# Attention and MoE on one core: scores for two token tiles at once, scale sums with 16-bit operands

## The chip, the core and the metric

The kernel runs on one core of a Trainium2 chip. The core has a matrix engine (TensorE, PE in the profile, its weight loads PEld), a vector engine (VectorE, DVE), an engine for functions and copies (ScalarE, ACT), a general one (GpSimd, POOL), and SyncE (SP), which here only issues DMAs. Each engine takes its instructions in order; semaphores order them among each other. Matmuls write PSUM, a small memory of eight banks. The metric is the device time in microseconds, the median of three runs.

## What is computed

```python
def _attn_ref(q, k, v, sampled_blocks):      # B, H, S, D = 4, 8, 768, 64; blocks of 32 tokens
    scores = 1/sqrt(D) * q @ k^T
    mask = near the diagonal | first/last block row or column | sampled blocks
    scores = where(mask, scores, -1e9)
    attn = exp(scores - max) ; attn /= sum(attn) + 1e-9
    return attn @ v

def _moe_ref(x, w_in, w_out, alpha):         # 3072 tokens, 512 -> 2048 -> 512
    h = x @ w_in
    g = max(h, 0) + alpha * min(h, 0)
    return g @ w_out
```

The output of the attention, heads side by side, is the input x of the second part. All inputs are float32.

## The kernel before

**High and low halves.** A float32 operand is scaled by a power of two and split into a 16-bit high part and a 16-bit low part, the rest. Three of the four products of two such operands are summed (high by high, high by low, low by high); the scores take all four. The power of two comes from a sum of squares: ACT squares and sums along the row (L379), a matmul with a matrix of ones (L472 for k, L549 for v, L859 and L868 for the two weights) adds over the 128 rows, and DVE cuts the result to its exponent (`pow2`, L370). These small matmuls have float32 operands.

**Attention.** A chunk is two tiles of 128 tokens of one batch element; a unit is a chunk and a pair of heads; a step is one tile and one head. There are 12 chunks, 48 units and 192 steps, four steps to a unit. For a unit `T["qt"]` holds q transposed: for each head and tile 128 rows, the upper 64 the high part and the lower 64 the low part of the 64 features (`q_pair`, L453, and `emit_q_hi`, `emit_q_lo`, L441 and L446, which write them side by side). `T["kt"]` holds k in the same way, `T["ks"]` with the halves swapped. `emit_s` (L577) makes the 128 by 768 scores of a step: q by kt gives high by high plus low by low, q by ks gives both cross products, each in two matmuls of 512 and 256 columns into one buffer of two PSUM banks. The pool `s` has two such buffers, used also by the value products (`emit_av`, L649) and the mask. DVE then adds the mask and takes the minimum (L596), ACT does the exponential (L603), the result is split (L383, L387, L391, L393, L394), transposed by a DMA that SP issues (L624), and multiplied with v; the 64 columns of each of two heads make one half of the value product's 128 output rows.

**MoE.** For each chunk eight blocks of products with w_in (`emit_up`, L1023), the activation on DVE (L1033, L1034), its split on ACT (L1039) and POOL (L1044), and products with w_out (`emit_down`, L1065). Before its first block all 32 tiles of weights have to be loaded, converted and scaled. They come as float32 and are brought to an integer layout first in three steps: `emit_n1` on DVE (L829), `emit_n2` on ACT (L834) or DVE (L836), `emit_n3` on DVE (L841).

**Order.** Every piece of work is an `Op` with a priority, a price in microseconds for each engine that may run it, and the buffers it takes and gives back. `Plan.run` (L101) plays the engines forward, gives each ready op, in order of priority, to the engine that minimises its wait plus `PREF` times its price, and so fixes engine and order of all instructions before the kernel is built. An op starts only when all buffers that it takes are free. The constants at the top (L28 to L37, L47) set priorities: `MOE_LAG` is how many steps the MoE work of a chunk is behind its attention, `LDP` how far ahead of its use a weight tile is loaded, `V_WA`, `W_WA`, `V_WB`, `W_WB` when weights are prepared, `PL_V` and `P_V` when v is loaded and split. `attend` (L749) makes the ops of a step, `values` (L774) those of a value product, `raw_to_f32` (L948) those of the weights' conversion.

Of the kernel before, what the change touches and what calls it, by code (L numbers as in the profile page):

```python
# [14 lines left out]
ALU = mybir.AluOpType  # L15
# [9 lines left out]
GSCALE = 2.0**-20  # L25
SB = 205 << 23
SIZES0 = [2, 2, 2]
MOE_LAG = 13.782  # L28
EARLY = 15.72
MOE_BOOST = 0.564  # L30
V_WA = -18.766
W_WA = 0.725
V_WB = 0.937
W_WB = 0.741
LDP = 18.136
PL_V = -22.686
P_V = -0.023  # L37
PL = "gv"
LD = 4
P_PE = 0  # L40
# [3 lines left out]
HALF = 0  # L44
WO_PE = 1
LEADL = 2
PREF = {"PE": 1.0, "DVE": 1.91, "ACT": 1.15, "POOL": 0.744, "SP": 1.0}  # L47
SLOW = 1.25
UNTIL = 140.0
Q_PE = 1  # L50
# [167 lines left out]
def attn_moe(ctx: ExitStack, tc: tile.TileContext, q, k, v, sampled, w_in, w_out, alpha, out):  # L218
# [21 lines left out]
    def wt(tag, shape, dt, name=None):  # L240
        return work.tile(shape, dt, tag=tag, name=name or tag, bufs=bufs[tag])
# [9 lines left out]
    def new_small(name, dt=F32, w=1, n=4):  # L251
        return sm.tile([P, w], dt, tag=name, name=name, bufs=n)

    ident = cpool.tile([P, P], F32, name="ident")
    make_identity(nc, ident)
    ones = cpool.tile([P, P], F32, name="ones")
    nc.vector.memset(ones, 1.0)
    warm = cpool.tile([P, 1], F32, name="warm")
    nc.scalar.activation(warm, ones[:, 0:1], AF.Exp)
# [70 lines left out]
    bias = cpool.tile([P, NT, S], BF16, name="bias")  # L330
    ident16 = cpool.tile([P, P], F16, name="ident16")
    nc.gpsimd.tensor_copy(ident16, ident)
    nident = cpool.tile([P, P], F16, name="nident")
    nc.gpsimd.tensor_scalar(nident, ident, -1.0, None, ALU.mult)

# [75 lines left out]

    kbuf, ksbuf, vbuf, qtbuf, ptbuf, xbuf = {}, {}, {}, {}, {}, {}
    o_av = {}
    o_s, o_kt, o_ks, o_v2, o_qt, o_cs, o_pt, o_x, o_sv = {}, {}, {}, {}, {}, {}, {}, {}, {}

    def load(e, dst, src):
        (nc.sync if e == "SP" else nc.scalar).dma_start(dst, src)
# [21 lines left out]
        nc.vector.tensor_scalar(cs, T["rk", b][:, a:z], T["uq", c], -(2.0**-100), ALU.mult, ALU.min)  # L439

    def emit_q_hi(e, c):  # L441
        n = chunks[c][2]
        T["qn", c] = wt("qn", [P, H * n, 2, D], F16)
        times(e, T["qn", c][:, :, 0, :], T["qf", c].rearrange("p h t d -> p (h t) d"), T["sq", c])

    def emit_q_lo(c):  # L446
        nat = T["qn", c]
        nc.vector.scalar_tensor_tensor(
            nat[:, :, 1, :], T["qf", c].rearrange("p h t d -> p (h t) d"), T["sq", c], nat[:, :, 0, :],
            ALU.mult, ALU.subtract,  # L450
        )

    def q_pair(u):  # L453
        c, hp = units[u]
        n = chunks[c][2]
        return T["qn", c][:, 2 * hp * n : 2 * (hp + 1) * n].rearrange("p g a d -> p g (a d)")

    def emit_q_t(u):
        n = chunks[units[u][0]][2]
# [3 lines left out]
        )  # L463

    def emit_k_sq(b, hp):
        T["kss", b, hp] = new_small("kss")
        squares(T["kf", b, hp].rearrange("p h e -> p (h e)"), T["kss", b, hp])

    def emit_k_norm(b, hp):
# [76 lines left out]
    def lane_max(tot, key):  # L546
        pool, tag, w = key
        bc = pool.tile([P, w], F32, tag=tag, name="bc")
        nc.tensor.matmul(bc[:, :P], tot.broadcast_to([P, P]), ident, start=True, stop=True)  # L549
        return bc  # L550

    def emit_v_tot(b):
        T["vtot", b] = new_small("vtot")
        nc.vector.tensor_reduce(T["vtot", b], T["vss", b], AX.X, ALU.add)

    def emit_v_bc(b):
# [20 lines left out]
    def emit_s(n):  # L577
        u, j = steps[n]
        c, hp = units[u]
        b, t0, w = chunks[c]  # L580
        h, i = divmod(j, w)
        T["sp", n] = ps_s.tile([P, S], F32, tag="s", name="sp")
        for x, key in ((0, "kt"), (1, "ks")):
            kt = T[key, b, hp].rearrange("p h t j -> p h (t j)")
            for a, z in ((0, 512), (512, S)):
                nc.tensor.matmul(  # L586
                    T["sp", n][:, a:z], T["qt", u][:, h, i, :], kt[:, h, a:z], start=(x == 0), stop=(x == 1)
                )

    def emit_bias(n):  # L590
# [89 lines left out]
    def prep_k(b, hp, prio, gate, pl):  # L680
        fb = plan.buf("vf")
        o = plan.op(pl, LQ, lambda e: emit_load_kv(e, ("kf", b, hp), k_nat[b][:, 2 * hp : 2 * hp + 2, :]),
                    gate, [fb], dma=1.3)
        o = plan.op(prio, {"ACT": 0.85}, lambda: emit_k_sq(b, hp), [o], [], [fb])
        ab = plan.buf("o" if b == 0 else "h")
        o = plan.op(prio - 4, {"PE": 0.5}, lambda: emit_k_norm(b, hp), [o], [ab])
        o = plan.op(prio - 4, {"DVE": 0.35}, lambda: emit_k_scale(b, hp), [o], [], [ab])
        T["o_rk", b, hp] = o
        nb = plan.buf("ph")
        o = plan.op(prio, MAX4, lambda e: emit_k_hi(e, b, hp), [o], [nb], [fb])  # L690
        o = plan.op(prio, LOW4, lambda e: emit_k_lo(e, b, hp), [o], [], [nb, fb])
        kbuf[b, hp], ksbuf[b, hp] = plan.buf("kt"), plan.buf("ks")
        if b == 0 and hp < K_PE:
            for x, d, kb in ((0, o_kt, kbuf), (1, o_ks, ksbuf)):
                d[b, hp] = []
                for h in range(2):
                    tb = plan.buf("o")
                    t = plan.op(prio - 2, {"PE": 0.4 + 0.4 * x}, lambda x=x, h=h: emit_k_pe(b, hp, x, h), [o], [tb, kb[b, hp]], [nb])
                    d[b, hp].append(plan.op(prio - 2, {"ACT": 0.85, "DVE": 0.9}, lambda e, x=x, h=h: emit_k_copy(e, b, hp, x, h), [t], [kb[b, hp]], [tb]))
            return  # L700
        o_kt[b, hp] = [plan.op(prio - 2, {"SP": 2.0}, lambda: emit_k_t(b, hp), [o], [kbuf[b, hp]], [nb], dma=2.3)]
        o_ks[b, hp] = [plan.op(prio - 2, {"SP": 1.5}, lambda e: emit_k_swap(e, b, hp), o_kt[b, hp],
                               [ksbuf[b, hp]], [kbuf[b, hp]], dma=1.3)]

    def prep_v(b, pl, prio, gate):
        fbs, sq = [], []
        for hp in range(NP):
            fb = plan.buf("vf")
            fbs.append(fb)
            o = plan.op(pl + 0.1 * hp, LQ,  # L710
                        lambda e, hp=hp: emit_load_kv(e, ("vf", b, hp), v_nat[b][:, 2 * hp : 2 * hp + 2, :]),
                        gate, [fb] + ([plan.buf("ld")] if b == 0 else []), dma=1.3)
            sq.append(plan.op(pl + 2 + 0.1 * hp, {"ACT": 0.85}, lambda hp=hp: emit_v_sq(b, hp), [o], [], [fb]))
        o = plan.op(prio - 4, {"DVE": 0.1}, lambda: emit_v_tot(b), sq)
        ab = plan.buf("o" if b == 0 else "h")
        o = plan.op(prio - 4, {"PE": 0.6}, lambda: emit_v_bc(b), [o], [ab])
        o_sv[b] = plan.op(prio - 4, {"DVE": 0.5}, lambda: emit_v_scale(b), [o], [], [ab])
        for hp in range(NP):
            vbuf[b, hp] = plan.buf("v2")
            p = prio + hp  # L720
            o = plan.op(p, MAX4, lambda e, hp=hp: emit_v_hi(e, b, hp), [o_sv[b]], [vbuf[b, hp]], [fbs[hp]])
            o_v2[b, hp] = plan.op(p, LOW4, lambda e, hp=hp: emit_v_lo(e, b, hp), [o], [], [vbuf[b, hp], fbs[hp]])

    def prep_q(c, prio, pl, gate):
# [7 lines left out]
        for a, z in [(a, a + 1) for a in range(NP)] if c == 0 else [(0, NP)]:  # L732
            o = plan.op(prio, {"DVE": 0.15}, lambda a=a, z=z: emit_cs(c, a, z), [sc] + [T["o_rk", b, hp] for hp in range(a, z)])
            for hp in range(a, z):
                o_cs[us[hp]] = o
        o = plan.op(prio, {"POOL": 0.3 + 1.1 * f, "ACT": 0.2 + 0.9 * f, "DVE": (0.1 + 0.57 * f, 0)},
                    lambda e: emit_q_hi(e, c), [sc], [nb], [fb])
        lo = plan.op(prio, {"DVE": (0.1 + 1.15 * f, 0)}, lambda: emit_q_lo(c), [o], [], [nb, fb])
        for u in us:
            p = prio if c == 0 else first[u] - 5  # L740
            qtbuf[u] = plan.buf("qt")
# [7 lines left out]
    def attend(n):  # L749
# [1 line left out]
        c, hp = units[u]  # L751
        b, t0, w = chunks[c]
        h, i = divmod(j, w)
        sb, eb, pb = plan.buf("s"), plan.buf("e"), plan.buf("ph")
        o_s[n] = o = plan.op(n, {"PE": 0.66}, lambda: emit_s(n), [o_qt[u], o_av.get(steps[max(n - 3, 0)][0] - 2)] + o_kt[b, hp] + o_ks[b, hp], [sb],
                             [qtbuf[u], kbuf[b, hp], ksbuf[b, hp]])
        o = plan.op(n - 1, {"DVE": 0.94}, lambda: emit_bias(n), [o, o_cs[u], o_bias[t0 + i]], [eb], [sb])
        o = plan.op(n - 1, {"ACT": 0.94}, lambda: emit_exp(n), [o], [], [eb])
        o = plan.op(n - 2, {"DVE": 0.3}, lambda: emit_rs(n), [o])
# [32 lines left out]
    ssc = cpool.tile([P, NG], F32, name="ssc")  # L792
    gsc_a = cpool.tile([P, NG // 2], F32, name="gsc_a")
    am1_a = cpool.tile([P, NF // 2], F32, name="am1_a")
    isum = cpool.tile([P, NG], F32, name="isum")
    osum = cpool.tile([P, NG], F32, name="osum")
    s_wi = cpool.tile([P, 1], F32, name="s_wi")
    s_wo = cpool.tile([P, 1], F32, name="s_wo")
    s_wia = cpool.tile([P, 1], F32, name="s_wia")
# [147 lines left out]

    def raw_to_f32(name, f, p, o, deps, bufs):  # L948
        o = plan.op(p, {"DVE": (0.4, 0)}, lambda: emit_n1(name, f, 0), [o] + deps, [], bufs)
        o = plan.op(p, {"ACT": 0.7, "DVE": (0.64, 0)}, lambda e: emit_n2(e, name, f, 0), [o], [], bufs)  # L950
        return plan.op(p, {"DVE": (0.64, 0)}, lambda: emit_n3(name, f, 0), [o], [], bufs)

    def prep_wi(f, p):
# [6 lines left out]
        hb = plan.buf("h")  # L960
        o = plan.op(p - 2, {"PE": 0.9}, lambda: emit_gram("wi", g), [n3wi[f - 1], n3wi[f]], [hb])
        o = plan.op(p - 2, {"DVE": 0.28}, lambda: emit_gram_max("wi", g), [o], [], [hb])
        o = plan.op(p - 2, {"PE": 0.4}, lambda: emit_g_norm(g), [o], [], [hb])
        gs.append(plan.op(p - 2, {"DVE": 0.27}, lambda: emit_g_scale(g), [o], [], [hb]))
        prev = o_wi.get(f - 2)
        sb = plan.buf("sid")
# [7 lines left out]
    def prep_wo(f, p):  # L974
# [10 lines left out]
            return  # L985
        x = f // HF
        hb = plan.buf("h")
        o = plan.op(p - 3, {"PE": 0.6}, lambda: emit_o_norm(x), osq[-HG:], [hb])
        o = plan.op(p - 3, {"DVE": 0.3}, lambda: emit_o_scale(x), [o], [], [hb])
        o_swo.append(o)  # L990
        if WO_PE > x:
# [158 lines left out]
    for b in range(B):  # L1150
# [8 lines left out]
        for c in cb:  # L1159
# [52 lines left out]
```

## Time and profile before

| | |
|---|---|
| median of three runs | 863.18 us (862.94 to 869.0) |
| profiled execution, its own time | 860.22 us |
| its span, first to last instruction | 858.2 us |
| mean granted TensorE clock | 0.974 |
| up products L1023, busy | 266.7 us, 2304 matmuls |
| down products L1065, busy | 374.4 us summed over both kinds, 1152 matmuls |
| scores L586, busy | 150.8 us, 768 matmuls |
| value products L659, busy | 109.0 us, 1728 matmuls |

A time on the page is that of one profiled execution. Busy times of one engine may overlap: a matmul's record lasts until its result has drained, while the next has long begun, so the spacing of the starts is what a stream of matmuls costs. A group's row gives line, engine, operation, output and inputs, shapes, count, busy time, mean of one in ns, and the idle time ahead of it with what ended that.

### The profile page before, as it was taken

How to read it: one execution, taken by the hardware profiler on the slowest of the kernel's cores; microseconds unless marked ns; L12 is line 12 of the kernel's file. 1: busy time of each engine (PE TensorE's matmuls, PEld its weight loads, DVE VectorE, ACT ScalarE, POOL GpSimd, SP SyncE). 2: the span in 40 equal slices, each digit the busy share in tenths (PEclk: the TensorE clock that was granted, in tenths of full speed). 3: DMA queues.
4: the chain of work that ended last, by engine and by line, in shares of the span. 5: the costliest groups of instructions: out<-in, count | busy, mean ns of one | idle time of the engine just before them, and what ended most of it. 6: DMA issues, size and time to landing. Idle time of an engine off the chain costs nothing.

```text
span 858.2 us, 16828 instructions
## 1 busy us (share of the span) xinstructions
PE 805.6 (94%) x6291; PEld 541.2 (63%) x6291; DVE 635.7 (74%) x1389; ACT 507.2 (59%) x867; POOL 543.4 (63%) x446
## 2 busy tenths in 40 slices
PE   4757767999999999999999999999999999999997
PEld 2424345666766767666776676767666666667664
DVE  4877788989768787796898786878797867763222
ACT  7997967865547666665356656655376555552111
POOL 5476556977767667665768674867676655753221
PEclk9887968999999999999999999999999999999999
DMA  9996688997998799949998949859999856756000
GB/s 312 297 304 129 153 174 164 178 176 141 220 183 172 146 159 200 179 91 176 195 176 154 173 88 238 158 114 202 203 161 157 164 111 117 119 108 102 1 25 25
DMA packets 386449, 136.13 MB, mean 159 GB/s; under 512 B 350628, under 2 KB 379328, under 8 KB 386368
## 3 DMA queue, kind: packets, MB, share of 16 engines
q1 hardware_dynamic: 369104, 117.22, 71.2%
q10 hardware_dynamic: 17200, 17.83, 7.2%
q8 instruction: 49, 0.80, 0.4%
q14 instruction: 32, 0.26, 0.1%
q0 software_dynamic: 64, 0.02, 0.0%
HBM read 35.67 MB, written 6.29 MB: 49 GB/s over the span
## 4 chain that ended last, share of the span: by engine, by line
PE 82%; ACT 7%; DVE 5%; issue 3%; POOL 2%; DMA 1%; POOLq 0%; ACTq 0%; DVEq 0%
PE o L1065 28%; PE h L1023 28%; PE sp L586 13%; PE av L659 12%; ACT wo L834 1%; DVE e L596 1%; ACT raw L834 1%; ACT e L603 1%; DMA qf<-in_q_dram 1%; ACT wi L931 1%; DVE wo L841 1%; DVE ph L391 1%; ACT ph L383 1%; POOL e L393 0%; POOL gl L1044 0%
## 5 line engine op out<-in xcount | busy, mean ns | idle before, releaser
L1023 PE MATMUL h<-x,wi 128*128 128x256 f16 x2304 | 266.7, 273 | 0.6 <-DVE g L1034 0.6
L1023 PEld LDWEIGHTS <-wi 128*128 128x128 f16 x2304 | 224.4, 98 | 40.5 <-issue 2.1
L603 ACT ACTIVATE e<-e,nm 128x768 f32<-128x768 f32 x192 | 178.9, 932 | 119.8 <-DVE nm L596 117.0
L1065 PE MATMUL o<-wo,gh 128*128 128x512 f16 x768 | 228.7, 380 | 0.0
L596 DVE CUSTOM_DVE_ANT_0 e<-sp,bias,cs 128x768 f32<-128x768 f32 x192 | 191.0, 1011 | 30.2 <-PE sp L586 26.1
L1044 POOL TENSOR_TENSOR gl<-g,gh 128x512 f16<-128x512 f32 x96 | 117.5, 1225 | 121.8 <-ACT gh L1039 91.5
L394 POOL TENSOR_TENSOR ph<-e,ph 128x768 f16<-128x768 f32 x96 | 172.9, 1801 | 8.0
L1065 PE MATMUL o<-wo,gl 128*128 128x512 f16 x384 | 145.7, 379 | 0.7 <-POOL gl L1044 0.6
L1039 ACT CAST gh<-g 128x512 f16<-128x512 f32 x96 | 59.1, 616 | 140.7 <-DVE g L1034 121.8
L393 POOL TENSOR_SCALAR e<-e,rs 128x768 f32<-128x768 f32 x96 | 101.5, 1057 | 37.1 <-ACT ph L383 30.2
L1033 DVE SCALAR_TENSOR_TENSOR g<-h,am 128x512 f32<-128x512 f32 x96 | 65.9, 686 | 77.9 <-PE h L1023 75.6
L1065 PEld LDWEIGHTS <-gh 128*128 128x128 f16 x768 | 73.9, 98 | 78.3 <-issue 2.8
L391 DVE SCALAR_TENSOR_TENSOR ph<-e,rs,ph 128x768 f16<-128x768 f32 x96 | 118.3, 1234 | 5.5 <-ACT ph L383 5.3
L387 POOL TENSOR_SCALAR ph<-e,rs 128x768 f16<-128x768 f32 x71 | 73.3, 1033 | 75.9 <-DVE rs L609 33.3
L659 PE MATMUL av<-pt,v 128*64 128x256 f16 x1728 | 109.0, 283 | 9.4 <-DVE nm L596 8.3
L383 ACT ACTIVATE ph<-e,rs 128x768 f16<-128x768 f32 x112 | 103.8, 928 | 21.2 <-DVE rs L609 10.0
L586 PEld LDWEIGHTS <-qt 128*128 128x128 f16 x768 | 73.8, 99 | 63.7 <-issue 12.7
L659 PEld LDWEIGHTS <-v 128*64 128x64 f16 x1728 | 94.8, 114 | 26.8 <-issue 15.4
L586 PE MATMUL sp<-kt,qt 128*128 128x512 f16 (+1 forms) x384 | 96.1, 332 | 8.7 <-DVE nm L596 7.5
L586 PE MATMUL sp<-ks,qt 128*128 128x512 f16 (+1 forms) x384 | 95.5, 331 | 0.0
L1034 DVE SCALAR_TENSOR_TENSOR g<-h,gsc,g 128x512 f32<-128x512 f32 x96 | 72.1, 751 | 3.4
L1065 PEld LDWEIGHTS <-gl 128*128 128x128 f16 x384 | 37.5, 98 | 46.8 <-POOL gl L1044 1.6
(141 smaller groups left out, 670.7 us busy)
## 6 DMA issues: line engine op xcount, KB each, us to landing
wo<-in_moe_w_in_dram SPq DMA_DIRECT2D x12, 512.0 KB, 6.1
raw<-in_moe_w_out_dram SPq DMA_DIRECT2D x12, 512.0 KB, 5.9
ks<-kt SPq DMA_DIRECT2D x30, 192.0 KB, 4.1
qf<-in_q_dram ACTq DMA_DIRECT2D x8, 512.0 KB, 5.3
out_dram<-ob SPq DMA_DIRECT2D x15, 256.0 KB, 2.7
kf<-in_k_dram ACTq DMA_DIRECT2D x9, 384.0 KB, 4.9
vf<-in_v_dram ACTq DMA_DIRECT2D x9, 384.0 KB, 5.1
pt<-ph SPq DMA_TRANSPOSE x192, 4.2
```

The lines of the kernel that those rows point to most:

```text
L383: nc.scalar.activation(dst, src, AF.Copy, scale=scale)
L387: nc.gpsimd.tensor_scalar(dst, src, scale, 1.0, ALU.mult, ALU.mult)
L391: nc.vector.scalar_tensor_tensor(dst, src, scale, hi, ALU.mult, ALU.subtract)
L393: nc.gpsimd.tensor_scalar(tmp, src, scale, 1.0, ALU.mult, ALU.mult)
L394: nc.gpsimd.tensor_tensor(dst, tmp, hi, ALU.subtract)
L586: nc.tensor.matmul(T["sp", n][:, a:z], T["qt", u][:, h, i, :], kt[:, h, a:z], start=(x == 0), stop=(x == 1))
L596: nc.vector.tensor_tensor_reduce(T["e", n], T["sp", n], bias[:, t0 + j % w, :], scale=T["cs", c][:, hp : hp + 1], scalar=3.0e38, op0=ALU.a ...
L603: nc.scalar.activation(T["e", n], T["e", n], AF.Exp, bias=T["nm", n], scale=-1.0, accum_out=T["su", n])
L659: nc.tensor.matmul(av[h * D : (h + 1) * D, : n * P], v2[:, h, t, vv, :], T["pt", u, h][:, pl * NT + t, :], start=(m == 0), stop=(m == len( ...
L1023: nc.tensor.matmul(ph[:, i, :], win(w, f, ct), x[:, ct, :], start=(m == 0), stop=(m == len(terms) - 1))
L1044: nc.gpsimd.tensor_tensor(T["gl", c, j], T["g", c, j], T["gh", c, j], ALU.subtract)
L1065: nc.tensor.matmul(T["o", c][t], g[:, i, t * P : (t + 1) * P], wout(w, f), start=(i == 0 and m == 0 and j in first_j), stop=(i == 1 and m ...
```

## The change

Scores: the two tiles of a chunk and head are done by one op. The parts of q are laid out as high, low, low, high for the two tiles, so that tile 0 has its high part in the upper 64 rows and tile 1 in the lower 64. The cross products keep all 128 rows (tile 0 with `ks`, tile 1 with `kt`). High by high then needs 64 rows only: tile 0 in the upper 64 rows with `kt`, tile 1 in the lower 64 rows with `ks`, their matmuls alternating. Low by low is dropped. The op takes both buffers of the pool `s` at once.

```diff
     def emit_q_hi(e, c):
-        n = chunks[c][2]
-        T["qn", c] = wt("qn", [P, H * n, 2, D], F16)
-        times(e, T["qn", c][:, :, 0, :], T["qf", c].rearrange("p h t d -> p (h t) d"), T["sq", c])
-
-    def emit_q_lo(c):
+        T["qn", c] = wt("qn", [P, H, 4, D], F16)
+        times(e, T["qn", c][:, :, 0:4:3, :], T["qf", c], T["sq", c])
+
+    def emit_q_lo(c, t):
         nat = T["qn", c]
         nc.vector.scalar_tensor_tensor(
-            nat[:, :, 1, :], T["qf", c].rearrange("p h t d -> p (h t) d"), T["sq", c], nat[:, :, 0, :],
-            ALU.mult, ALU.subtract,
+            nat[:, :, 1 + t, :], T["qf", c][:, :, t, :], T["sq", c], nat[:, :, 3 * t, :], ALU.mult, ALU.subtract
         )
...
-        h, i = divmod(j, w)
-        T["sp", n] = ps_s.tile([P, S], F32, tag="s", name="sp")
-        for x, key in ((0, "kt"), (1, "ks")):
-            kt = T[key, b, hp].rearrange("p h t j -> p h (t j)")
-            for a, z in ((0, 512), (512, S)):
+        h = j // 2
+        halves = ((0, 512), (512, S))
+        kt, ks = (T[x, b, hp].rearrange("p h t j -> p h (t j)") for x in ("kt", "ks"))
+        for i in range(2):
+            T["sp", n + i] = ps_s.tile([P, S], F32, tag="s", name="sp")
+            for a, z in halves:
                 nc.tensor.matmul(
-                    T["sp", n][:, a:z], T["qt", u][:, h, i, :], kt[:, h, a:z], start=(x == 0), stop=(x == 1)
+                    T["sp", n + i][:, a:z], T["qt", u][:, h, i, :], (ks, kt)[i][:, h, a:z], start=True, stop=False
+                )
+        for a, z in halves:
+            for i in range(2):
+                r = slice(D * i, D * i + D)
+                nc.tensor.matmul(
+                    T["sp", n + i][:, a:z], T["qt", u][r, h, i, :], (kt, ks)[i][r, h, a:z], start=False, stop=True
                 )
...
-        lo = plan.op(prio, {"DVE": (0.1 + 1.15 * f, 0)}, lambda: emit_q_lo(c), [o], [], [nb, fb])
+        for t in range(2):
+            lo = plan.op(prio, {"DVE": (0.1 + 0.58 * f, 0)}, lambda t=t: emit_q_lo(c, t), [o], [], [nb, fb])
+            o = lo
...
-        sb, eb, pb = plan.buf("s"), plan.buf("e"), plan.buf("ph")
-        o_s[n] = o = plan.op(n, {"PE": 0.66}, lambda: emit_s(n), [o_qt[u], o_av.get(steps[max(n - 3, 0)][0] - 2)] + o_kt[b, hp] + o_ks[b, hp], [sb],
-                             [qtbuf[u], kbuf[b, hp], ksbuf[b, hp]])
+        eb, pb = plan.buf("e"), plan.buf("ph")
+        if i == 0:
+            sbuf[n], sbuf[n + 1] = plan.buf("s"), plan.buf("s")
+            o_s[n] = o_s[n + 1] = plan.op(n, {"PE": 1.17}, lambda: emit_s(n), [o_qt[u], o_av.get(steps[max(n - 3, 0)][0] - 2)] + o_kt[b, hp] + o_ks[b, hp],
+                                          [sbuf[n], sbuf[n + 1]], [qtbuf[u], kbuf[b, hp], ksbuf[b, hp]])
+        o, sb = o_s[n], sbuf[n]
```

Scale sums: the ones, the sums of squares and the identity of these matmuls become bf16; `identb` is a bf16 copy of the identity made by POOL at the start.

```diff
-    ones = cpool.tile([P, P], F32, name="ones")
+    ones = cpool.tile([P, P], BF16, name="ones")
...
-        T["kss", b, hp] = new_small("kss")
+        T["kss", b, hp] = new_small("kss", BF16)
...
-        nc.tensor.matmul(bc[:, :P], tot.broadcast_to([P, P]), ident, start=True, stop=True)
+        nc.tensor.matmul(bc[:, :P], tot.broadcast_to([P, P]), identb, start=True, stop=True)
...
-    isum = cpool.tile([P, NG], F32, name="isum")
-    osum = cpool.tile([P, NG], F32, name="osum")
+    isum = cpool.tile([P, NG], BF16, name="isum")
+    osum = cpool.tile([P, NG], BF16, name="osum")
```

The planner: new constants, a higher price for the second step of the weights' conversion on ACT, and lower prices for the scale sums on PE (0.5 to 0.15, 0.6 to 0.2, 0.4 to 0.15 and 0.6 to 0.25).

```diff
-MOE_LAG = 13.782
+MOE_LAG = 10.618
...
-MOE_BOOST = 0.564
+MOE_BOOST = 1.211
...
-W_WA = 0.725
-V_WB = 0.937
-W_WB = 0.741
-LDP = 18.136
-PL_V = -22.686
-P_V = -0.023
+W_WA = 0.754
+V_WB = 1.134
+W_WB = 0.607
+LDP = 30.529
+PL_V = -33.326
+P_V = 0.73
...
-PREF = {"PE": 1.0, "DVE": 1.91, "ACT": 1.15, "POOL": 0.744, "SP": 1.0}
+PREF = {"PE": 1.0, "DVE": 1.896, "ACT": 1.009, "POOL": 0.778, "SP": 1.0}
...
-        o = plan.op(p, {"ACT": 0.7, "DVE": (0.64, 0)}, lambda e: emit_n2(e, name, f, 0), [o], [], bufs)
+        o = plan.op(p, {"ACT": 1.29, "DVE": (0.64, 0)}, lambda e: emit_n2(e, name, f, 0), [o], [], bufs)
```

More of the change, by code (lines that the diff above doesn't have):

```diff
@@ L332, in attn_moe @@
     nc.gpsimd.tensor_copy(ident16, ident)
+    identb = cpool.tile([P, P], BF16, name="identb")
+    nc.gpsimd.tensor_copy(identb, ident)
     nident = cpool.tile([P, P], F16, name="nident")
@@ L413, in attn_moe @@
     o_av = {}
-    o_s, o_kt, o_ks, o_v2, o_qt, o_cs, o_pt, o_x, o_sv = {}, {}, {}, {}, {}, {}, {}, {}, {}
+    o_s, o_kt, o_ks, o_v2, o_qt, o_cs, o_pt, o_x, o_sv, sbuf = {}, {}, {}, {}, {}, {}, {}, {}, {}, {}
     def load(e, dst, src):
@@ L454, in q_pair @@
         c, hp = units[u]
-        n = chunks[c][2]
-        return T["qn", c][:, 2 * hp * n : 2 * (hp + 1) * n].rearrange("p g a d -> p g (a d)")
+        return T["qn", c][:, 2 * hp : 2 * hp + 2].rearrange("p h (g a) d -> p (h g) (a d)", a=2)
     def emit_q_t(u):
@@ L548, in lane_max @@
         bc = pool.tile([P, w], F32, tag=tag, name="bc")
-        nc.tensor.matmul(bc[:, :P], tot.broadcast_to([P, P]), ident, start=True, stop=True)
+        nc.tensor.matmul(bc[:, :P], tot.broadcast_to([P, P]), identb, start=True, stop=True)
         return bc
     def emit_v_tot(b):
-        T["vtot", b] = new_small("vtot")
+        T["vtot", b] = new_small("vtot", BF16)
         nc.vector.tensor_reduce(T["vtot", b], T["vss", b], AX.X, ALU.add)
@@ L579, in emit_s @@
         c, hp = units[u]
-        b, t0, w = chunks[c]
-        h, i = divmod(j, w)
-        T["sp", n] = ps_s.tile([P, S], F32, tag="s", name="sp")
-        for x, key in ((0, "kt"), (1, "ks")):
-            kt = T[key, b, hp].rearrange("p h t j -> p h (t j)")
-            for a, z in ((0, 512), (512, S)):
-                nc.tensor.matmul(
-                    T["sp", n][:, a:z], T["qt", u][:, h, i, :], kt[:, h, a:z], start=(x == 0), stop=(x == 1)
+        b = chunks[c][0]
+        h = j // 2
[4 more added lines that the diff above has]
+            for a, z in halves:
+                nc.tensor.matmul(
+                    T["sp", n + i][:, a:z], T["qt", u][:, h, i, :], (ks, kt)[i][:, h, a:z], start=True, stop=False
[5 more added lines that the diff above has]
+                    T["sp", n + i][:, a:z], T["qt", u][r, h, i, :], (kt, ks)[i][r, h, a:z], start=False, stop=True
                 )
@@ L685, in prep_k @@
         ab = plan.buf("o" if b == 0 else "h")
-        o = plan.op(prio - 4, {"PE": 0.5}, lambda: emit_k_norm(b, hp), [o], [ab])
+        o = plan.op(prio - 4, {"PE": 0.15}, lambda: emit_k_norm(b, hp), [o], [ab])
         o = plan.op(prio - 4, {"DVE": 0.35}, lambda: emit_k_scale(b, hp), [o], [], [ab])
@@ L715, in prep_v @@
         ab = plan.buf("o" if b == 0 else "h")
-        o = plan.op(prio - 4, {"PE": 0.6}, lambda: emit_v_bc(b), [o], [ab])
+        o = plan.op(prio - 4, {"PE": 0.2}, lambda: emit_v_bc(b), [o], [ab])
         o_sv[b] = plan.op(prio - 4, {"DVE": 0.5}, lambda: emit_v_scale(b), [o], [], [ab])
@@ L962, in prep_wi @@
         o = plan.op(p - 2, {"DVE": 0.28}, lambda: emit_gram_max("wi", g), [o], [], [hb])
-        o = plan.op(p - 2, {"PE": 0.4}, lambda: emit_g_norm(g), [o], [], [hb])
+        o = plan.op(p - 2, {"PE": 0.15}, lambda: emit_g_norm(g), [o], [], [hb])
         gs.append(plan.op(p - 2, {"DVE": 0.27}, lambda: emit_g_scale(g), [o], [], [hb]))
@@ L987, in prep_wo @@
         hb = plan.buf("h")
-        o = plan.op(p - 3, {"PE": 0.6}, lambda: emit_o_norm(x), osq[-HG:], [hb])
+        o = plan.op(p - 3, {"PE": 0.25}, lambda: emit_o_norm(x), osq[-HG:], [hb])
         o = plan.op(p - 3, {"DVE": 0.3}, lambda: emit_o_scale(x), [o], [], [hb])
@@ L1173, in attn_moe @@
             moe(c)
+    ctx.enter_context(nc.allow_low_precision(reason="sums that only choose a power of two"))
     for o in plan.run():
```

## The prediction

> **What bounds the kernel now.** I read the page's busy line, its slices and its chain first, then the busy time in two windows, then the waits of TensorE.
>
> ```profile
> span 858.2 us, 16828 instructions
> PE 805.6 (94%) x6291; PEld 541.2 (63%) x6291; DVE 635.7 (74%) x1389; ACT 507.2 (59%) x867; POOL 543.4 (63%) x446
> PE   4757767999999999999999999999999999999997
> PE 82%; ACT 7%; DVE 5%; issue 3%; POOL 2%; DMA 1%; POOLq 0%; ACTq 0%; DVEq 0%
> ```
> TensorE is busy 94% of the span, and 82% of the chain that ended last is its own. The slices show two stages: some 150 us in which nothing is full, then nines to the end. The two windows (PE, PEld, DVE, ACT, POOL busy us, then granted clock, DMA share, GB/s) and the only wait of TensorE after 160 us say it exactly:
>
> ```profile
> 0.00:160.00 160.00, 112.17 (x699) 68.47 (x700) 122.21 (x292) 131.31 (x199) 97.80 (x95) 0.86 0.86 215
> 160.00:860.00 700.00, 693.41 (x5595) 472.77 (x5592) 513.51 (x1097) 375.89 (x668) 445.62 (x352) 1.00 0.77 145
> PE o L1065 <- POOL gl L1044: 0.6, 1, 0.6
> ```
> After 160 us TensorE waits 0.6 us in all and runs at the full granted clock. What it saves there comes off the end, as long as DVE (513.5 of some 698 us) and DMA (0.77) keep pace. Before 160 us it idles 160 - 112.2 = 47.8 us; there ACT (131 of 160) and DVE (122) set the pace, and a cheaper score saves nothing.
>
> **The scores.** The score groups after 160 us (PE, PEld), and a stretch of TensorE's timeline, whose first column is the start:
>
> ```profile
> 160.00:860.00 700.00, 124.41 (x652) 62.12 (x652) 1.00 0.77 145
> ```
> ```profile
> 603.18 2.78 PE L1023 MATMUL h<-x,wi 128*128 128x256 f16 x24
> 605.80 0.28 PE L472 MATMUL tot<-kss,ones 128*128 128x1 f32 x2
> 605.95 0.59 PE L1065 MATMUL o<-wo,gh 128*128 128x512 f16 x2
> ...
> 608.53 0.49 PE L586 MATMUL sp<-kt,qt 128*128 128x512 f16 x2
> 608.86 0.49 PE L586 MATMUL sp<-ks,qt 128*128 128x512 f16 x2
> 609.18 0.49 PE L586 MATMUL sp<-kt,qt 128*128 128x512 f16 x2
> 609.51 0.49 PE L586 MATMUL sp<-ks,qt 128*128 128x512 f16 x2
> 609.83 2.78 PE L1023 MATMUL h<-x,wi 128*128 128x256 f16 x24
> 612.55 2.16 PE L659 MATMUL av<-pt,v 128*64 128x256 f16 x36
> 614.63 0.50 PE L586 MATMUL sp<-kt,qt 128*128 128x512 f16 x2
> ```
> Durations overlap, so I go by starts. Two token tiles take 609.83 - 608.53 = 1.30 us: four passes of 0.325 over 768 columns. The new pair has one cross pass per tile (2 x 0.325 = 0.65), then the high by high products: two passes of 64 rows each, that may run at once. Nothing in this trace splits the array by rows, but the value products split it by columns (128*64), and 36 of them take 614.63 - 612.55 = 2.08 us. The 24 full products of the same 256 columns from 603.18 take 2.62 us, 0.109 each, so 36 in a row would be 3.93: the two halves do run at once, as 18 products of 0.109 (1.97) plus 0.11. Entering costs too: the 24 products from 609.83 need 2.72 until the first value product starts, 0.10 more than the 24 from 603.18. So changing to half tiles and back costs 0.10 + 0.11 = 0.21 us per visit. Carried over to rows: 0.65 + 0.325 + 0.21 = 1.185, a saving of 0.115 per pair.
>
> The bounds: 0.975 if the row split changes for nothing (saving 0.325), and 0.65 + 0.65 + 0.21 = 1.51 if the halves run one after the other (a loss of 0.21). I take 1.185, since the value products are the nearest row and show both the overlap and the change. After 160 us there are 652 / 4 = 163 steps, 81.5 pairs: 81.5 x 0.115 = 9.4 us off. The bounds are 26.5 off and 17.1 on. The 29 steps before 160 us count for nothing: TensorE idles there.
>
> **The scale sums.** f32 pairs of matmuls become one 16-bit matmul. From the rows above, a `tot` pair holds TensorE 605.95 - 605.80 = 0.15 us. After 160 us stand:
>
> ```profile
> 160.00:860.00 700.00, 3.57 (x24) 3.85 (x24) 1.00 0.77 145
> 160.00:860.00 700.00, 1.16 (x6) 0.91 (x6) 1.00 0.77 145
> ```
> The first row is L472, 12 pairs, the second L549, 3 pairs. All of it together holds TensorE at most 12 x 0.15 + 3 x 0.25 = 2.6 us (0.25 as two 128-column passes of about 0.11 by the 0.109 above, rounded up). I take 1.3 off, half of it, because one of two passes goes; ends 0 and 2.6. The other such sums (L859, L868) lie in the idle stage: nothing. The identity's 16-bit copy is one more instruction on POOL at the very start; POOL is busy 97.8 of the first 160 us, which hides it.
>
> **Low part of q, in two instructions.**
>
> ```profile
> L448 DVE SCALAR_TENSOR_TENSOR qn<-qf,sq,qn 128x1024 f16<-128x1024 f32 x12 | 20.8, 1737 | 0.4 <-ACT qn L383 0.4
> ```
> Twelve of 1.74 us become 24 of half the elements. I add 0.1 us of fixed cost each, 1.2 us of DVE in all, hidden by DVE's free quarter after 160 us; in the worst case, without that cover, 1.2 us. The SP transposes of q keep their count and size; only the order of parts within a group changes.
>
> **The order.** Prices, priorities and weights of the planner change, so every queue is reshuffled. The telling rows of the first stage (windows 0 to 140 of all engines and of L834 on ACT, a group, three waits, the first MoE matmul):
>
> ```profile
> 0.00:140.00 140.00, 93.97 (x535) 54.42 (x537) 103.72 (x255) 117.14 (x175) 81.04 (x83) 0.84 0.89 226
> 0.00:140.00 140.00, 39.65 (x30) 0.84 0.89 226
> L836 DVE SCALAR_TENSOR_TENSOR wo<-raw,wo 128x512 int32<-128x512 int32 x2 | 1.4, 682 | 0.0
> POOL sid L915 <- DVE ssc L374: 16.3, 3, 7.5
> DVE wi L841 <- ACT wo L834: 6.2, 9, 1.5
> DVE wo L841 <- ACT raw L834: 5.2, 6, 1.7
> 142.40 0.82 PE L1023 MATMUL h<-x,wi 128*128 128x256 f16 x6
> ```
> The second step of the weights' conversion runs 30 times on ACT at 39.65 / 30 = 1.32 us and twice on DVE at 0.68. The old plan priced ACT's at 0.7, the new at 1.29. With the preferences the planner weighed 1.15 x 1.05 x 0.7 = 0.85 against 1.91 x 1.08 x 1.25 x 0.64 = 1.65 for DVE; now 1.009 x 1.05 x 1.29 = 1.37 against 1.64. So DVE wins as soon as ACT's queue is 0.27 us longer, not 0.8. I guess that 12 move: ACT 15.8 us less, DVE 8.2 more, 7.6 less in sum, 3.8 for each of two engines that are busy 84% and 74%. I take 3 us off the time to the MoE's first matmul. Against it: the 32 weight loads (priority now about -49 instead of -37) go ahead of k's second to fourth load and of v's on the SP and ACT queues, where the DMA share is already 0.89, so the first attention steps come later; and the smaller MoE_LAG puts MoE work ahead of scores earlier. The ends I give this: 10 off (a fifth of the 47.8 idle) and 8 on (about the longest single wait, 7.5).
>
> **The price of pairing.** A pair needs both score buffers free, and the value products use the same two. Two softmax first steps in a row on DVE:
>
> ```profile
> 499.80 1.00 DVE L596 CUSTOM_DVE_ANT_0 e<-sp,bias,cs 128x768 f32<-128x768 f32 x1
> 500.73 0.09 DVE L596 DVE_READ_ACCUMULATOR2_ANT nm<- 128x1 f32 x1
> 500.73 1.01 DVE L596 CUSTOM_DVE_ANT_0 e<-sp,bias,cs 128x768 f32<-128x768 f32 x1
> ...
> L670 ACT ACTIVATE x<-av 128x256 f16<-128x256 f32 x48 | 18.2, 380 | 30.2 <-PE av L659 30.1
> L675 DVE SCALAR_TENSOR_TENSOR x<-av,x 128x256 f16<-128x256 f32 x48 | 20.1, 420 | 20.0 <-ACT x L670 19.6
> ```
> A step empties its buffer in 0.93 us, so a pair holds both for 1.19 + 1.87 = 3.06 us at least, and the values for 2.08 + 0.38 + 0.42 = 2.88. A group of four steps and one value product needs 2 x 3.06 + 2.88 = 9.0 us of this chain, strictly one after the other; it has some 700 / 40.75 = 17.2. Half is slack, filled with MoE products, so I charge 1 us; ends 0 and the rival below.
>
> **Sum.** The profiled execution took 860.2, 2.0 over its span. 860.2 - 9.4 - 1.3 - 3.0 + 1.0 = 847.5. The median of the three runs, 863.2, stands 3.0 higher, so the forecast is 850.5.
>
> **Rivals.**
> (a) The row halves overlap badly. For it: no row shows a split by rows. Against it: the column halves overlap fully. One after the other, the scores add 17.1 where I took 9.4 off: 850.5 + 26.5 = 877; overlapping for half of their time (0.49 for 0.325, the pair 1.35), they add 4.1: 864. The saving is gone at a high part of 0.44 (0.65 + 0.44 + 0.21 = 1.30). With no row for it and the nearest one against it, I give 0.07 to the first and 0.05 to the second. The Trainium skill's page "TensorE: Matmul & The Clock Gate", in its part on packing small matmuls, has 3.07 times measured for four row tiles, not 4; an estimate by that share makes the high part 0.42 and the time 858. No run here shows a row split; the value products, at full overlap, speak against it.
> (b) The paired buffers stall TensorE: it reaches a pair in its own order while DVE is still at the second softmax step, and everything behind it on TensorE waits. For it: DVE is busy 513.5 of 698 and takes its work in order. Each such wait is about 0.93. The gain of 13.7 without the 1 us charged is gone at 13.7 / 81.5 = 0.17 us per pair, that is at one pair in 5.5; at one in two (38 us) the time is 888, at one in four (19 us) 868. Against it: the slack above, and the 0.6 us of waits in 700 now. The skill's page "TensorEngine Tiling (Array Packing)", under PSUM pressure, says that row tiles need different banks and raise the pressure; that is this case. I give it 0.13.
> (c) The new order loses in the first stage what the scores win: 8 on instead of 3 off, 861. 0.09.
> (d) The change of tiling is free: 0.325 saved per pair, 17.1 more than the sum: 833. Against it stand the 0.10 and 0.11 around each value product. The same tiling page states, among its key properties, that changing the mode drains the engine; the trace agrees with 0.21 us. 0.06.
>
> **How the numbers follow.** My own case, 842 to 858, has 0.60; (a) 0.12, (b) 0.13, (c) 0.09, (d) 0.06. One per cent is 8.6 us, about what a measurement of this kernel can tell from no change (its three runs span 862.9 to 869.0): faster means under 854.6, slower over 871.8. Faster: 0.53 of my case, (d), and 0.03 of the light ends of (a) and (b): 0.62. Slower: 0.07 of (a) and 0.06 of (b): 0.13. The rest, 0.25, is the same. Leaving out (d) and the heavy ends of (a) and (b), the range is 836 to 867.
>
> **What would show it.** Right: score pairs that follow each other at 1.15 to 1.22 us by their starts, with pairs of 64-row matmuls starting at almost the same time; no wait of TensorE on L596 worth 2 us in sum after the first stage; fewer conversions on ACT and a first MoE matmul near 139. Wrong: 1.3 to 1.5 us a pair (a); idle time of TensorE before scores in the second stage, released by the softmax's first step (b); a first MoE matmul after 150, or gaps in the slices past the eighth (c).

## The result and the profile after

The changed kernel takes 840.8 us (839.9 to 842.7), the kernel before 863.5 in the same runs: a ratio of 0.9727, with a 95% interval of 0.9684 to 0.977. The profiled execution took 840.9 us, at the median this time. The page, busy line, slices and chain:

```profile
span 839.1 us, 16792 instructions
PE 787.2 (94%) x6255; PEld 497.9 (59%) x6255; DVE 648.7 (77%) x1403; ACT 506.6 (60%) x868; POOL 549.3 (65%) x442
PE   4767759999999999999999999999999999999997
PE 79%; DVE 11%; issue 4%; DMA 3%; ACT 2%; POOL 2%; POOLq 0%; DVEq 0%; ACTq 0%
```
TensorE still bounds the kernel, and the nines begin a slice earlier. The two windows, and what TensorE waited for after 160 us:

```profile
0.00:160.00 160.00, 113.81 (x748) 61.61 (x749) 141.52 (x315) 126.02 (x199) 105.33 (x101) 0.90 0.96 223
160.00:860.00 700.00, 673.39 (x5509) 436.30 (x5506) 507.17 (x1089) 380.54 (x670) 444.02 (x342) 1.00 0.77 143
PE sp L586 <- DVE nm L602: 0.9, 2, 0.4
```
The second stage remains saturated: 839.1 - 160 - 673.4 = 5.7 us without a matmul, 4.8 before, some 4 of them at the end when only the output is left. A score pair in TensorE's timeline, with a scale sum ahead of it:

```profile
603.20 0.17 PE L471 MATMUL tot<-kss,ones 128*128 128x1 bf16 x1
603.23 2.78 PE L1034 MATMUL h<-x,wi 128*128 128x256 f16 x24
...
610.63 0.49 PE L586 MATMUL sp<-ks,qt 128*128 128x512 f16 x2
610.96 0.49 PE L586 MATMUL sp<-kt,qt 128*128 128x512 f16 x2
611.38 0.39 PE L592 MATMUL sp<-kt,qt 64*128 64x512 f16 x1
611.38 0.39 PE L592 MATMUL sp<-ks,qt 64*128 64x512 f16 x1
611.60 0.27 PE L592 MATMUL sp<-kt,qt 64*128 64x256 f16 x1
611.61 0.27 PE L592 MATMUL sp<-ks,qt 64*128 64x256 f16 x1
611.81 2.79 PE L1034 MATMUL h<-x,wi 128*128 128x256 f16 x24
```
The pair takes 611.81 - 610.63 = 1.18 us. Both halves start together (611.38, 611.60). From 610.96 to 611.38 there are 0.42 us for a pass of 0.325, and from the last 256-column pair to the next product 0.20 us for 0.11: 0.10 and 0.09 for the change of tiling.

**Where 19.1 us of span went.** What was still to be done at 160 us tells the first stage from the second. Counts of down products and value products, first two rows before, next two after, then the cross matmuls of the scores after:

```profile
160.00:860.00 700.00, 264.63 (x1152) 111.23 (x1152) 1.00 0.77 145
160.00:860.00 700.00, 92.71 (x1548) 81.17 (x1548) 1.00 0.77 145
...
160.00:860.00 700.00, 258.65 (x1126) 103.98 (x1123) 1.00 0.77 143
160.00:860.00 700.00, 90.56 (x1512) 79.27 (x1512) 1.00 0.77 143
160.00:860.00 700.00, 66.53 (x324) 31.69 (x324) 1.00 0.77 143
```
By 160 us the changed kernel is ahead by 26 down products of 0.216 us (5.6), one value product of 36 matmuls (2.1), one step (163 left before, 324 / 4 = 81 pairs now: 0.65) and five up products of 0.109 (2213 left before, 2208 now: 0.5): 8.9 us from the first stage. The 81 pairs save 0.12 each, 9.7. A sum of k costs 603.23 - 603.20 = 0.03 instead of 0.15, 12 times: 1.4; the sums of v fell from 1.16 us busy to

```profile
160.00:860.00 700.00, 0.69 (x3) 0.29 (x3) 1.00 0.77 143
```
that is 0.5 less. Idle time took 0.9 back. 8.9 + 9.7 + 1.4 + 0.5 - 0.9 = 19.6, half a microsecond more than the difference of 858.2 and 839.1.

The first stage itself (window 0 to 140 of all engines; ACT's conversions; DVE's low part of q; the first MoE product):

```profile
0.00:140.00 140.00, 94.27 (x573) 48.63 (x574) 122.43 (x276) 111.16 (x172) 86.80 (x87) 0.89 0.99 232
0.00:140.00 140.00, 29.26 (x22) 0.89 0.99 232
L449 DVE SCALAR_TENSOR_TENSOR qn<-qf,sq,qn 128x512 f16<-128x512 f32 x24 | 24.9, 1043 | 1.2 <-ACT qn L385 1.2
134.85 1.38 PE L1034 MATMUL h<-x,wi 128*128 128x256 f16 x11
```
Ten conversions on DVE where it was two, 22 on ACT where it was 30; DVE is now the fuller engine with 122 of 140 us, and the MoE starts 142.4 - 134.9 = 7.5 us earlier.

### The profile page after: what moved, and what is told of

The parts are those of the page before. It is cut to its first block, busy times and chain, and to the rows that moved or that the text cites. A ratio compares the mean times of both kernels' runs of the same rounds, so it can differ in the third digit from the quotient of the medians.

```text
span 839.1 us, 16792 instructions
## 1 busy us (share of the span) xinstructions
PE 787.2 (94%) x6255; PEld 497.9 (59%) x6255; DVE 648.7 (77%) x1403; ACT 506.6 (60%) x868; POOL 549.3 (65%) x442
## 4 chain that ended last, share of the span: by engine, by line
PE 79%; DVE 11%; issue 4%; DMA 3%; ACT 2%; POOL 2%; POOLq 0%; DVEq 0%; ACTq 0%
PE o L1076 28%; PE h L1034 27%; PE av L665 11%; PE sp L586 6%; PE sp L592 4%; DVE e L602 3%; DVE ph L393 2%; PE d L937 1%; DVE wo L852 1%; DVE wi L840 1%; DMA kf<-in_k_dram 1%; DMA pt<-ph 1%; DMA raw<-in_moe_w_out_dram 1%; POOL v L389 1%; DVE wi L852 1%
## 5 line engine op out<-in xcount | busy, mean ns | idle before, releaser
L1034 PEld LDWEIGHTS <-wi 128*128 128x128 f16 x2304 | 220.5, 98 | 48.0 <-issue 15.2
L396 POOL TENSOR_TENSOR ph<-e,ph 128x768 f16<-128x768 f32 x96 | 179.3, 1868 | 8.0
L389 POOL TENSOR_SCALAR ph<-e,rs 128x768 f16<-128x768 f32 x70 | 76.5, 1094 | 104.1 <-ACT e L609 63.3
L393 DVE SCALAR_TENSOR_TENSOR ph<-e,rs,ph 128x768 f16<-128x768 f32 x96 | 123.5, 1288 | 6.8 <-ACT ph L385 4.0
L385 ACT ACTIVATE ph<-e,rs 128x768 f16<-128x768 f32 x117 | 108.2, 930 | 24.1 <-ACT e L609 7.7
L1076 PEld LDWEIGHTS <-gh 128*128 128x128 f16 x768 | 69.1, 98 | 86.6 <-issue 15.9
L395 POOL TENSOR_SCALAR e<-e,rs 128x768 f32<-128x768 f32 x96 | 95.8, 998 | 34.4 <-ACT ph L385 30.5
L586 PEld LDWEIGHTS <-qt 128*128 128x128 f16 x384 | 37.2, 99 | 46.2 <-issue 13.8
L586 PE MATMUL sp<-kt,qt 128*128 128x512 f16 x192 | 47.8, 331 | 8.3 <-DVE nm L602 7.8
L586 PE MATMUL sp<-ks,qt 128*128 128x512 f16 x192 | 47.9, 332 | 7.5 <-DVE nm L602 7.5
```

Of the source, the lines that this page charges most:

```text
L385: nc.scalar.activation(dst, src, AF.Copy, scale=scale)
L389: nc.gpsimd.tensor_scalar(dst, src, scale, 1.0, ALU.mult, ALU.mult)
L393: nc.vector.scalar_tensor_tensor(dst, src, scale, hi, ALU.mult, ALU.subtract)
L395: nc.gpsimd.tensor_scalar(tmp, src, scale, 1.0, ALU.mult, ALU.mult)
L396: nc.gpsimd.tensor_tensor(dst, tmp, hi, ALU.subtract)
L586: nc.tensor.matmul(T["sp", n + i][:, a:z], T["qt", u][:, h, i, :], (ks, kt)[i][:, h, a:z], start=True, stop=False)
```

## The experiments

**Order and scores, each alone.** e1 is the one before with the new constants and this line:

```diff
-        o = plan.op(p, {"ACT": 0.7, "DVE": (0.64, 0)}, lambda e: emit_n2(e, name, f, 0), [o], [], bufs)
+        o = plan.op(p, {"ACT": 1.29, "DVE": (0.64, 0)}, lambda e: emit_n2(e, name, f, 0), [o], [], bufs)
```


> The kernel before with the planner's new constants and the new price of the conversion's second step alone; scores and scale sums as before. Theory: the new order brings the first MoE matmul forward by some 7 us and so 8.8 us of the gain, whatever the scores do: 863.5 - 9 = 854.5, first MoE matmul near 135. Rival: the scores and sums bring the first stage forward themselves, and the order is worth nothing without them: 863, first MoE matmul near 142.

863.7 us, ratio 1.002 (0.9987 to 1.005), first MoE matmul at 143.05, with eight conversions on DVE: worth nothing without the new scores. e2 is its counterpart, the changed kernel with the constants and the line of before.

> The changed kernel with the old constants and the old price of the conversion's second step. Theory: scores (9.7) and sums (1.8) keep their worth after the first stage, which is as long as before: 863.5 - 11.5 = 852, first MoE matmul near 142. Rival: the scores also shorten the first stage: 843, first MoE matmul near 135.

852.8 us, 0.988 (0.9849 to 0.991), the figure of the theory, but not for its reason. The first MoE matmul came at 137.9, earlier than before, and the second stage gave it back: between 160 us and the end TensorE was busy

```profile
160.00:860.00 700.00, 676.36 (x5533) 437.57 (x5531) 518.67 (x1100) 363.53 (x654) 456.52 (x356) 1.00 0.78 144
PE sp L586 <- DVE x L681: 3.4, 4, 1.4
PE av L665 <- DVE nm L602: 3.3, 3, 1.6
PE sp L586 <- DVE nm L602: 1.9, 4, 0.8
```
of 850.9 - 160 = 690.9, idle for 14.5 us where the changed kernel idles for 5.7. The waits stand before scores and value products, for DVE to empty a score buffer. Against the kernel before, TensorE has 693.4 - 676.4 = 17.0 us less to do after 160 us. Scores and sums are 11.6 of this, so 5.4 come from the first stage, though the constants and the price are the old ones; and it idles 14.5 - 4.8 = 9.7 us longer. So scores and order do not add up: 0 and -10.8 alone, -22.7 together.

**The row halves.** e3 is the changed kernel with the same plan, but 128 rows in the last products:

```diff
-                r = slice(D * i, D * i + D)
...
-                    T["sp", n + i][:, a:z], T["qt", u][r, h, i, :], (kt, ks)[i][r, h, a:z], start=False, stop=True
+                    T["sp", n + i][:, a:z], T["qt", u][:, h, i, :], (kt, ks)[i][:, h, a:z], start=False, stop=True
```


> The changed kernel with the high by high products over all 128 rows (low by low is back in the sum), everything else the same. Theory: no half tiles, so no change of tiling and no overlap; a pair costs 1.30 for 1.18 us, 81 pairs after the first stage: 840.8 + 9.7 = 850.5. Rival: the pair's gain comes from its being one op, not from the row halves: 841.

852.0 us, 0.9868 (0.9836 to 0.99), 11.2 more than the changed kernel. Its pair:

```profile
620.02 0.49 PE L586 MATMUL sp<-ks,qt 128*128 128x512 f16 x2
620.34 0.49 PE L586 MATMUL sp<-kt,qt 128*128 128x512 f16 x2
620.67 0.38 PE L591 MATMUL sp<-kt,qt 128*128 128x512 f16 x1
620.88 0.38 PE L591 MATMUL sp<-ks,qt 128*128 128x512 f16 x1
621.10 0.27 PE L591 MATMUL sp<-kt,qt 128*128 128x256 f16 x1
621.21 0.27 PE L591 MATMUL sp<-ks,qt 128*128 128x256 f16 x1
621.32 2.78 PE L1033 MATMUL h<-x,wi 128*128 128x256 f16 x24
```
1.30 us, no change of tiling at either end, and 0.11 us between the last matmul's start and the next product. The halves are worth what was forecast for them, 9.7. In the profiled execution, TensorE is busy for 684.0 us after 160 us, 10.6 more than in the changed kernel: the 9.7, and about 1 for two down products and ten matmuls of value products that were left. It idles 1.2 us longer.

**Another order of the halves.** e4 is the changed kernel, tile by tile instead of column part by column part:

```diff
-        for a, z in halves:
-            for i in range(2):
+        for i in range(2):
+            for a, z in halves:
```


> The changed kernel with the 64-row products in another order: both column parts of tile 0, then both of tile 1. Theory: halves overlap only with their neighbour in the order, so 512 columns, then 256 beside 512: 0.54 for 0.325 us, the pair 1.40: 840.8 + 81 x 0.215 = 858. Rivals: they overlap in any order, 841; not at all, 867.

842.6 us, 0.9751 (0.9716 to 0.9785), the same as the changed kernel. My theory, that halves overlap only with their neighbour, falls:

```profile
614.24 0.39 PE L592 MATMUL sp<-kt,qt 64*128 64x512 f16 x1
614.25 0.39 PE L592 MATMUL sp<-ks,qt 64*128 64x512 f16 x1
614.47 0.27 PE L592 MATMUL sp<-kt,qt 64*128 64x256 f16 x1
614.48 0.27 PE L592 MATMUL sp<-ks,qt 64*128 64x256 f16 x1
614.68 0.28 PE L1034 MATMUL h<-x,wi 128*128 128x256 f16 x1
```
In the program `kt` 512, `kt` 256, `ks` 512, `ks` 256 follow each other, and a loop at the kernel's end makes every instruction depend on the one before it on its engine (`add_manual_dep`), so this is the order in which TensorE gets them. On the chip `ks` 512 starts 0.01 us after `kt` 512 and 0.22 ahead of `kt` 256, which precedes it in the program; all 96 pairs of the run start in this order.

**The scale sums.** e5 is the kernel before with 16-bit operands alone, e6 the changed kernel with float32 operands alone. Planner prices stay in both, and so does the plan.

```diff
-    ones = cpool.tile([P, P], F32, name="ones")
+    ones = cpool.tile([P, P], BF16, name="ones")
...
-    isum = cpool.tile([P, NG], F32, name="isum")
-    osum = cpool.tile([P, NG], F32, name="osum")
+    isum = cpool.tile([P, NG], BF16, name="isum")
+    osum = cpool.tile([P, NG], BF16, name="osum")
```


> The kernel before with 16-bit operands in the scale sums alone; planner prices and constants as before, so engines and order stay the same. Theory: only TensorE time after the first stage counts: 12 x 0.11 + 3 x 0.16 = 1.8 us, 863.5 - 1.8 = 861.7. Rival: the sums stand in the latency chains of the first stage (waits of DVE ku on PE tot, POOL sid on DVE ssc) and bring the first MoE matmul forward by 4 us or more: 858 or less.

864.3 us, 1.0008 (0.9984 to 1.0031): no gain to be seen; 1.8 us is too little for these runs to tell. The first MoE matmul came at 148.3, 5.9 us later than in the kernel before, against the rival. ACT waited 4.5 us for a load of v there, and at most 0.1 in the kernel before. Whether the sums or the loads made the difference, one execution doesn't tell; the plan did not, so starts that lie some 6 us apart needn't come from a plan.

> The changed kernel with float32 operands in the scale sums again, planner as changed, so the order stays that of the changed kernel. Theory: 840.8 + 1.8 = 842.6. Rival, sums in the chain of the first stage: 845 or more, first MoE matmul after 138.

845.6 us, 0.977 (0.9743 to 0.9798), 4.8 more than the changed kernel, with the first MoE matmul at 136.2. The rival's 845 is met, its 138 is not, and the old kernel does not bear it out. Three executions with this plan and 16-bit sums (the changed kernel, e3, e4) start the MoE at 134.5 to 134.9. Inconclusive: the sums are worth something between nothing and 5 us.

**The price.** e7 is the changed kernel with 0.7 in the line of the first diff.

> The changed kernel with the old price of 0.7 for the conversion's second step on ACT. Theory: the price is what shortens the first stage; with 30 of 32 steps on ACT again the first MoE matmul is near 139 and the time 845. Rival: price and place of this step do not matter, 841.

852.7 us, 0.9859 (0.9837 to 0.9882). ACT's conversions and the first MoE matmul:

```profile
0.00:140.00 140.00, 39.26 (x30) 0.83 0.92 225
144.00 1.26 PE L1034 MATMUL h<-x,wi 128*128 128x256 f16 x10
```
Thirty of 32 are on ACT again, and the stage is 9 us longer, more than twice what I expected. e9 has the new price alone in the old kernel:

> The kernel before with the new price of the conversion's second step on ACT alone. Taking that price back in the changed kernel cost 11.8 us. Theory: the price is worth as much in the old kernel: first MoE matmul near 135, 854. Rival: what an order is worth depends on all that it is made for, and no constant has a worth of its own: anything from 858 to 868.

860.7 us, 0.999 (0.9963 to 1.0017). The first MoE matmul moved to 137.2, but the time did not follow beyond noise. In the profiled execution TensorE has 689.2 us left to do after 160 us, 4.2 less than in the kernel before, and idles for 858.2 - 160 - 689.2 = 9.0, 4.2 more: the second stage gave it back. So the price has no worth of its own: 11.8 us in one plan, nothing that can be told in the other.

**Lag.** e8 is e2 with two of the new constants:

```diff
-MOE_LAG = 13.782
+MOE_LAG = 10.618
...
-MOE_BOOST = 0.564
+MOE_BOOST = 1.211
```


> The changed kernel with all old constants and the old price, but the new MOE_LAG and MOE_BOOST. The same with the old ones too took 852.8 and left TensorE idle for 10.5 us after 160 us, in front of scores and value products that waited for a score buffer. Theory: MOE_LAG and MOE_BOOST, which put MoE work ahead of more scores, remove these waits: idle after 160 us under 4, time near 845. Rival: the waits follow from other constants (PREF, the places of v and of the weights) and stay: 850 or more.

852.4 us, 0.9858 (0.9827 to 0.9888): a miss; 848.8 - 160 - 676.1 = 12.7 us idle in the second stage where it was 14.5 (the 10.5 above, and the 1.7 below, leave out the 4 us at the end). From the other side comes e12, the changed kernel with one constant moved:

```diff
-MOE_LAG = 10.618
+MOE_LAG = 12.2
```


> The changed kernel with MOE_LAG 12.2 for 10.618, scores put ahead of MoE work by 1.6 more steps. If the lag keeps TensorE from waiting for score buffers, its idle time after 160 us rises from 1.7 us to 4 or more and the time to 843 or more; if it does not matter, 841, and any change of more than 2 us comes from the first stage.

857.3 us, 0.9929 (0.9909 to 0.9949): 16.5 more, nearly three quarters of the gain. The first MoE matmul is at 136.4, and 1128 down products are left at 160 us, so the first stage is almost the same. Idle time in the second stage is 856.2 - 160 - 679.8 = 16.4 us for 5.7, and this is where it comes from (a wait in sum; then pieces of the timeline of TensorE, ACT and DVE; then four short windows with busy time and granted clock):

```profile
PE sp L586 <- DVE x L681: 6.7, 4, 3.9
...
253.95 0.16 PE L471 MATMUL tot<-kss,ones 128*128 128x1 bf16 x1 [1.60 <-ACT junk L381]
255.94 3.44 PE L665 MATMUL av<-pt,v 128*64 128x256 f16 x36 [1.82 <-DVE nm L602]
259.31 0.50 PE L586 MATMUL sp<-ks,qt 128*128 128x512 f16 x2
260.27 0.36 ACT L676 ACTIVATE x<-av 128x256 f16<-128x256 f32 x1
260.94 2.39 DVE L393 SCALAR_TENSOR_TENSOR v<-vf,sv,v 128x768 f16<-128x768 f32 x1
263.25 0.41 DVE L681 SCALAR_TENSOR_TENSOR x<-av,x 128x256 f16<-128x256 f32 x1
263.72 0.82 PE L586 MATMUL sp<-kt,qt 128*128 128x512 f16 x2 [3.91 <-DVE x L681]
265.23 4.54 PE L1034 MATMUL h<-x,wi 128*128 128x256 f16 x24
269.61 0.49 PE L586 MATMUL sp<-ks,qt 128*128 128x512 f16 x2
...
256.00:258.00 2.00, 2.00 (x20) 1.68 (x22) 1.22 (x5) 2.00 (x5) 1.92 (x2) 0.50 1.04 321
260.00:262.00 2.00, 0.00 (x0) 0.00 (x0) 2.00 (x2) 0.63 (x2) 1.92 (x2) 1.00 1.18 196
264.00:266.00 2.00, 2.00 (x10) 0.71 (x9) 0.67 (x1) 0.00 (x0) 0.00 (x0) 0.50 1.33 187
269.00:270.00 1.00, 1.00 (x11) 0.80 (x9) 0.19 (x1) 0.00 (x0) 0.92 (x2) 1.00 0.93 191
```
The value product holds one of the two score buffers. Tile 0 of the pair takes the free one at 259.31; tile 1 needs the other, which DVE empties at L681 only after 2.39 us of preparing v. TensorE stands for 3.91 us, with the MoE products queued behind the pair. It began earlier: TensorE had stood for 1.60 us at a scale sum of k, whose squares ACT began only at 252.97, behind two output copies, and for 1.82 before the value product, until DVE had read a score buffer.

The granted clock falls twice: to 0.50 after these two shorter waits, and, after 1.00 from 260 to 262, to 0.50 again around the end of the long one. The value product that the first fall meets takes 259.31 - 255.94 = 3.37 us for 2.08, and the block of 24 products after the second 269.61 - 265.23 = 4.38 for 2.62. In e2, with no such wait over 1.6 us, the clock stays at 1.00; what wait it takes to bring it down, these runs don't say. So of the 17.1 us that its span is longer, 10.7 are idle time and 3.1 the loss of these two at the lower clock; about 1.6 are work left at 160 us (two down products, 20 matmuls of value products).

**Nudges.** A constant that only shifts when weights are prepared, moved by 0.03 in the changed kernel (e10) and in the one before (e11, from 0.725 to 0.755).

```diff
-W_WA = 0.754
+W_WA = 0.784
```


> The changed kernel with W_WA 0.784 for 0.754, a nudge that has no meaning beyond another order of the weights' preparation. Theory: the changed kernel's order is one good draw among many, and a nudge costs some us: first MoE matmul 136 to 142, 843 to 850. Rival: the short first stage is robust, 840 to 842.

851.0 us, 0.9869 (0.983 to 0.9907): 10.2 more than the changed kernel. Its first MoE product:

```profile
146.28 2.79 PE L1034 MATMUL h<-x,wi 128*128 128x256 f16 x24
```
It is 11.4 us later; the second stage idles for 6.5 us, hardly more than 5.7.

> The kernel before with W_WA 0.755 for 0.725, the same nudge. Theory of draws: 860 to 872, first MoE matmul anywhere from 140 to 150. Rival: robust, 862 to 865.

866.4 us, 1.0041 (1.0016 to 1.0066), with the first MoE matmul at 139.1. Slower although the MoE starts earlier: the start alone does not say how much work is done by 160 us (696.1 us are left here, 693.4 before).

None of these versions beats the changed kernel.

## Why the prediction held, and what in it was off

The direction, the range (836 to 867) and the mechanism of the scores held: 840.8 us, faster by more than 1%. The likeliest time, 850.5, was 9.7 too long, for these reasons:

- Scores: 9.4 off forecast, 9.7 measured. The pair was to cost 1.185 and costs 1.18; the overlap and the change of tiling, read from the value products' column halves, carry over to row halves as they stand. Rival (a) and rival (d) fall with it. e3, with the same plan, confirms the size on the chip.
- Scale sums: 1.3 forecast, 1.9 by the trace after 160 us. I took half off, for one of two passes; more than half goes. By starts k's fell from 0.15 to 0.03 us and v's from 0.22 to 0.07. The 0.25 that I took for v's was misread, since the 0.109 behind it is a product of 256 columns and not of 128; it came near the 0.22 by luck. The two runs on the sums alone don't settle what they do beyond that.
- Pairing: 1.0 charged, 0.9 more idle time measured. But rival (b) is real, not remote: with the old order it took 14.5 - 5.7 = 8.8 us more idle time, with MOE_LAG at 12.2 it took 10.7 and a lowered clock. Most of it are waits before scores and value products for a score buffer: 8.6 us in e2 and 9.0 in e12, 0.9 in the changed kernel, none in the kernel before, whose constants e2 has. I weighed only DVE's second softmax step; the worst wait was for the value product's buffer behind a long DVE instruction. The average slack I argued from, 9.0 of 17.2 us, was not to the point: single late pairs cost, not the mean.
- Order: the mis-sized term. I took 3 us off the time to the MoE's first matmul; it came 7.5 us earlier, at 134.9 instead of 139, and the first stage gave 8.9 us. That it came out a gain at all was luck as far as these runs show. My reason was that fewer conversions on ACT start the MoE earlier. Eight moved where I guessed twelve; ACT lost 6.0 us of the first 140 and DVE gained 18.7, not 8.2. And the number on ACT does not set the start: with 30 there it came at 137.0 to 148.3 (the kernel before, e2, e5, e7, e8, e11), with 22 to 24 at 134.5 to 146.3 (the changed kernel, e1, e3, e4, e6, e9, e10, e12). The size was not to be had that way either: e10 takes 10.2 us away with a nudge, e7 11.8 with the price, and e1 shows the same constants to be worth nothing with the old scores. A price change was treated as a saving that adds to the others; the runs show a plan to be one draw, in which all parts act together.
- I put the scores before 160 us at nothing, since TensorE idles there. That may not hold for the plan: e2, with the old constants, has 5.4 us less left at 160 us beside what scores and sums save after it. One execution can't tell this from the 6 us that e5 shows without a change of plan.
- The rest, 2.8 us, is mostly the step from the profiled execution to the median: 3.0 added because the profile before was 3.0 under its median, while the profile after lies on it.
- Low part of q: 24 x 1.04 = 24.9 us for 20.8, 4.1 more on DVE instead of 1.2. After 160 us TensorE waits for none of them.

What stays open is what makes a plan's first stage short, and why the new order does so only together with the new scores. e2 (old order, new scores, 137.9) and e9 (old scores, new price, 137.2) each start the MoE early, e1 with both constants and price does not; but e5 shows that single starts of one plan in the old kernel can lie some 6 us apart.

## What to carry to other kernels

Price a new use of the matrix engine from the nearest one in the same trace, by the spacing of starts, with the change into it and out of it: 0.10 and 0.09 us a visit here, more than half of the 0.325 us that the row halves save. Where two PSUM buffers serve both a paired product and another, look at the longest instruction that can stand before the one that empties them, not at the mean; a lag that puts other work between is part of the change. When a planner's constants change with the code, treat its effect as a draw with a spread (a nudge cost 10 us in the changed kernel and 3 in the one before) and measure nudges of it before giving any single constant the credit.

## What the runs showed of the hardware

Matmuls on the two row halves need not start in the order of the program. In e4 the second tile's 512 columns start 0.22 us ahead of the first tile's 256, which stand before them, and so in all 96 pairs. The Trainium skill's page "TensorE: Matmul & The Clock Gate", in its part on packing small matmuls, states that matmuls keep program order in start and end, a strict first in, first out. For the starts this trace differs, and the measurement decides: each half went through its own two matmuls in order, beside the other. Of the ends nothing can be said, since the profile models them.
